# Splits, transposes and exchange of a four-head unit, each three steps further behind its loads

## The chip, the cores and the metric

The kernel runs on one core of a Trainium2 chip. The metric is the device time of one execution in microseconds (us); the times shown for a kernel are the median, lowest and highest of several runs. A trace of one execution shows for each engine (PE for matmuls, with its weight loads apart; DVE, ACT and POOL for elementwise work; SP, which here only issues DMAs) when each instruction ran and what it waited for.

## The reference

Block-causal attention over 8 batches of 8 heads with 576 positions of 64 elements, and behind it a mixture of experts in which each of the 4608 tokens goes to one of 8 experts.

```python
scores = scale * np.matmul(q, k.transpose(0, 1, 3, 2))
mask = block_i >= block_j                       # blocks of 64 positions
scores = np.where(mask, scores, -1000000000.0)
attn = softmax(scores)
x = np.matmul(attn, v)                          # then (batch*seq, heads*dim) = (4608, 512)

logits = x @ w_gate
e_idx = np.argmax(logits, axis=1)               # one expert for each token
eom = 1.0 / (1.0 + np.exp(-(x @ w_output_gate)))
for e in range(E):                              # 8 experts, w1 512x1024, w2 1024x512
    h = np.maximum(x[mask] @ w1[e], 0.0)
    out[mask] = gate_w[mask, None] * eom[mask, e, None] * (h @ w2[e])
```

## The kernel before

Attention comes first, the experts' matmuls after it. Attention goes through 32 *pairs* of heads (p = 0 to 31, four to a batch). For each pair the main loop (lines 936 to 964) calls `advance`, which weaves three generators: the scores and exponentials of pair p (`softmax`), the PE transposes of the probabilities of pair p-1 (`flip`), and the products with the values of pair p-2 (`values`). `weave_` (line 282) lets each generator take one step in turn, and after them each generator in the list `later`. `flip` has seven yields and so eight steps, hence a pair is eight *steps* long. The order on PE is the order in which these steps are written (a manual schedule). The instructions of the other engines and of the DMA queues are put in order by a planner at build time, which takes whatever its own model of the machine has ready, in the order of the program where several things are.

The q and k rows come in *units* of four heads (u = 0 to 15, two pairs each); unit u is first needed in the first step of pair 2u. The chain that prepares one unit is the class `Load` (lines 80 to 112):

- `fetch` (line 91): two DMAs of 576 KB on SP's queue, k and q, into two `nat` tiles (four buffers).
- `split(i)` (lines 96, 97): DVE casts `nat` to f16, POOL subtracts that from `nat` for the low part; both parts lie in one `sp` tile (two buffers).
- `turn(i)` (line 102): a DMA transpose on SP's queue, `sp` into `tr`.
- `swap` (lines 107, 108): two DMAs on SP's queue that copy the two halves of the transposed k crosswise into `sw`, the operand of the second score matmul (line 318).

`load_heads(u)` issues this chain. It is put into `later` at pair 2u-3 (for the last unit, 15, at pair 26), so it has three pairs, 24 steps, until its unit is needed. Its first step issues the fetch; an entry t of the tuple in line 123 means that the piece is issued in step t+1. Step 1 is in pair 2u-3, step 9 is the first of pair 2u-2, step 17 the first of pair 2u-1.

What else stands in SP's queue around these: `load_v` (line 293), called at the end of each pair, which issues four DMAs for that pair's values (`va` line 299, two for `vb` line 301, `v8` line 304; in the profile `v8` is `v`); and the stores of the attention rows `x_d` (line 460) of `finish_batch`, twelve further steps in `later` that run from pair 4b+6 on for batch b. The last step of `finish_batch` issues five scatters of the routing table on POOL (line 558). `load_first` (line 777) fetches and splits the weights of the first expert and gathers its tokens; it is put into `later` at the first pair that starts with all 16 units complete (line 948) and needs 24 steps. Unit 0 and unit 1 are prepared by `load_start`, with steps of its own.

Of the kernel before, what the change touches and what calls it, by code (L numbers as in the profile page):

```python
# [26 lines left out]
def block_attention_top1_moe(  # L27
# [86 lines left out]
    def load_heads(u):  # L114

        x = Load(u)
        x.fetch()
        todo = (
            lambda: x.split(0, nc.vector.tensor_copy, nc.gpsimd), lambda: x.split(1, nc.vector.tensor_copy, nc.gpsimd),
            lambda: x.turn(0), lambda: x.turn(1), x.swap,  # L120
        )
        at = 0
        for t, do in zip((4, 5, 8, 9, 13), todo):
            while at < t:
                at += 1
                yield
            do()
        x.done()
# [782 lines left out]


    loads = {2 * u - (4 if u == len(units) - 1 else 3): load_heads(u) for u in range(2, len(units))}
    loads[0] = start
    flips, prods = [], []
# [184 lines left out]
```

## Time and profile before

| | us |
|---|---|
| median of 3 runs | 831.13 |
| lowest, highest | 830.74, 835.34 |
| the profiled execution | 833.94 |
| its span, first to last instruction | 832.3 |
| PE busy in the span | 765.9 (92%) |
| DVE busy | 542.4 (65%) |
| ACT busy | 516.2 (62%) |
| POOL busy | 254.5 (31%) |

A row of a timeline in the sections below reads: start in us, length in us, engine, line, operation, output <- inputs, count; in square brackets stands how long the engine was idle before the row, and what ended that. A row of the waits reads: the engine and what it was about to do, <- what it waited for: us in total, times, longest. "SPq" is SP's queue, and its lengths are times of issue, not of the transfer. A row of the windows gives the stretch, its length, the busy time of PE, weight loads, DVE, ACT and POOL with the number of instructions in brackets, then the clock granted to PE (1.00 is full), the busy share of the DMA engines and GB/s. Attention takes the span up to about 402 us, the experts the rest.

### The profile page before, as it was taken

The numbers are of one execution on the slowest core, as the hardware profiler recorded it, in microseconds if no ns is written. First come the engines' busy times: TensorE is split into PE (matmuls) and PEld (weight loads), VectorE is DVE, ScalarE is ACT, GpSimd is POOL, SyncE is SP. The second block draws the span as 40 slices with busy tenths as digits, with TensorE's granted clock in tenths as the row PEclk, the third lists the DMA queues.
The fourth block names the chain that finished last, engine by engine and source line by source line (L and its number), as shares of the span: only waits on it lengthen the run. The fifth ranks groups of instructions, "written<-read, shape, count | busy, mean of one in ns | idle before, by whom it ended". The sixth has DMA issues, their size and how long they took to land. (4 is left out here: it accounts for less than half of the span.)

```text
span 832.3 us, 17653 instructions
## 1 busy us (share of the span) xinstructions
PE 765.9 (92%) x6430; PEld 512.0 (62%) x6430; DVE 542.4 (65%) x1192; ACT 516.2 (62%) x1206; POOL 254.5 (31%) x227
## 2 busy tenths in 40 slices
PE   4399997999899989788999999999999999999994
PEld 3266665656566656555676666676656666676652
DVE  5466874958587777858581866786566656786530
ACT  4478686776767767458512855775555555775530
POOL 4322142422324242437225542233122322210001
PEclk9789999999999999889999999999999999999998
DMA  8999989689689898995118699784789958832601
GB/s 156 177 181 169 188 119 174 154 177 221 137 170 189 152 186 172 201 233 165 41 59 278 157 278 328 240 253 101 236 267 296 291 172 251 192 52 58 225 30 41
DMA packets 258414, 149.13 MB, mean 179 GB/s; under 512 B 226960, under 2 KB 227024, under 8 KB 258320
## 3 DMA queue, kind: packets, MB, share of 16 engines
q1 hardware_dynamic: 250048, 128.64, 67.3%
q0 software_dynamic: 8272, 19.29, 7.4%
q8 instruction: 52, 0.85, 0.5%
q14 instruction: 42, 0.34, 0.1%
HBM read 122.23 MB, written 19.73 MB: 171 GB/s over the span
## 5 line engine op out<-in xcount | busy, mean ns | idle before, releaser
L873 PEld LDWEIGHTS <-w1b 128*128 128x128 f16 (+1 forms) x2112 | 182.7, 98 | 23.4 <-DVE w1b L762 1.5
L337 ACT ACTIVATE pt<-ps_s,nbs 128x448 f32<-128x448 f32 (+1 forms) x314 | 163.9, 531 | 34.1 <-DVE nbs L325 16.9
L873 PE MATMUL ps_s<-xt,w1b 128*128 128x256 f16 (+3 forms) x1824 | 182.1, 261 | 0.3 <-DVE w1b L762 0.2
L900 PE MATMUL ps_t<-w2b,hh 128*128 128x512 f16 x608 | 181.0, 379 | 1.3 <-ACT hh L881 1.3
L762 DVE TENSOR_TENSOR w2b<-w2f,w2b 128x1024 bf16<-128x1024 f32 x76 | 88.0, 1220 | 113.3 <-ACT w2b L761 113.3
L413 ACT COPY pT<-ps_t 128x512 f32<-128x512 f32 (+3 forms) x225 | 97.5, 461 | 74.9 <-PE ps_t L407 73.8
L407 PE MATMUL ps_t<-ident,pt 128*128 128x128 f32 (+1 forms) x800 | 128.9, 286 | 5.8 <-DVE xn L456 4.4
L97 POOL TENSOR_TENSOR sp<-nat,sp 128x1152 f16<-128x1152 f32 x30 | 71.2, 2375 | 147.6 <-DVE nbs L325 71.4
L900 PE MATMUL ps_t<-w2b,hl 128*128 128x512 f16 x304 | 115.2, 379 | 0.1
L317 PE MATMUL ps_s<-tr,tr 128*128 128x448 f16 (+1 forms) x378 | 100.0, 287 | 15.6 <-ACT pt L337 12.7
L903 ACT ACTIVATE ys<-ps_t,ids 128x512 f32<-128x512 f32 x38 | 26.1, 688 | 135.0 <-PE ps_t L900 115.6
L318 PE MATMUL ps_s<-sw,tr 128*128 128x448 f16 (+1 forms) x378 | 92.4, 286 | 13.3 <-DMA sw<-tr 13.2
L900 PEld LDWEIGHTS <-hh 128*128 128x128 f16 x608 | 59.2, 98 | 68.2 <-ACT hh L881 1.5
L904 POOL DMA_INDIRECT out_dram<-ys,ids x38 | 44.1, 1162 | 184.6 <-ACT ys L903 120.4
L407 PEld LDWEIGHTS ps_t<-ident,pt 128*128 128x128 f32 (+1 forms) x800 | 88.5, 144 | 18.7 <-DVE xn L456 4.8
L762 DVE TENSOR_TENSOR w1b<-w1f,w1b 128x1024 bf16<-128x1024 f32 x76 | 88.3, 1221 | 1.0 <-ACT w1b L761 0.7
L422 PE MATMUL ps_a<-pT,va 128*64 128x512 f32 (+3 forms) x256 | 84.5, 453 | 3.8 <-DMA va<-in_v_dram 3.6
L422 PE MATMUL ps_a<-pT,vb 128*64 128x512 f32 (+3 forms) x256 | 84.4, 453 | 1.0 <-DMA vb<-in_v_dram 1.0
L375 DVE TENSOR_REDUCE nmx<-ps_s 128x2 f32<-128x896 f32 (+1 forms) x63 | 60.2, 956 | 35.3 <-PE ps_s L320 35.0
L761 ACT CAST w1b<-w1f 128x1024 f16<-128x1024 f32 x76 | 74.4, 1045 | 2.6 <-DMA w1f<-in_moe_w_dram 2.6
L761 ACT CAST w2b<-w2f 128x1024 f16<-128x1024 f32 x76 | 73.6, 1042 | 0.0
L733 POOL DMA_INDIRECT xg<-x_d,ids x38 | 50.1, 1317 | 48.4 <-DMA ids<-tab_d 21.8
(196 smaller groups left out, 1084.7 us busy)
## 6 DMA issues: line engine op xcount, KB each, us to landing
w1f<-in_moe_w_dram SPq DMA_DIRECT2D x76, 512.0 KB
w2f<-in_moe_w_dram SPq DMA_DIRECT2D x76, 512.0 KB
nat<-in_k_dram SPq DMA_DIRECT2D x15, 576.0 KB
nat<-in_q_dram SPq DMA_DIRECT2D x15, 576.0 KB
sw<-tr SPq DMA_DIRECT2D x30, 288.0 KB
x_d<-xn SPq DMA_DIRECT2D x32, 256.0 KB
va<-in_v_dram SPq DMA_DIRECT2D x32, 128.0 KB
vb<-in_v_dram SPq DMA_DIRECT2D x64, 64.0 KB
```

The lines of the kernel that those rows point to most:

```text
L97: last_lo[0] = lo.tensor_tensor(sp[:, :, 1, :], self.nats[i], sp[:, :, 0, :], ALU.subtract)
L317: nc.tensor.matmul(ps_ap, qq, k1[ab][:, c0:c1], start=True, stop=False)
L318: nc.tensor.matmul(ps_ap, qq, k2[ab][:, c0:c1], start=False, stop=last)
L337: last_exp[0] = nc.scalar.activation(to, ap, AF.Exp, bias=nbs[0:r, t, ab:ab + 1], scale=SCALE, accum_out=sums[0:r, t, hA + ab:hA + ab + 1],)
L375: nc.vector.tensor_reduce(nmx[:, t, :], pX[:, :, 0:n], AX.X, ALU.max, negate=True)
L407: nc.tensor.transpose(ps[:, i, 0:rows], probs[t][0:rows, col:col + P], ident[0:rows, 0:rows])
L413: copies[next(nth)](pT[:, r:r + m, Q0[t]:Q0[t] + rows], ps[:, i:i + m, 0:rows])
L422: nc.tensor.matmul(pa[64 * a:64 * a + 64, P * j:512], (va, vb)[a][:, j, :], pT[:, 1 + 2 * j + a, 64 + P * j:576], start=(j == 0), stop=False,)
L761: nc.scalar.copy(hi, src)
L762: eng.tensor_tensor(lo, src, hi, ALU.subtract)
L873: nc.tensor.matmul(ph[:, f4].rearrange("p (h n) -> p h n", n=P), wv[:, cc, f, :], xv[:, cc], start=(k == 0), stop=(k == 3 * KD - 1))
L900: nc.tensor.matmul(py, hv[:, f, h], wv[:, f, :], start=(k == 0), stop=(k == 3 * KF - 1))
```

## The change

The tuple of steps in `load_heads` is changed: every piece behind the fetch is issued three steps later.

```diff
             lambda: x.turn(0), lambda: x.turn(1), x.swap,
         )
         at = 0
-        for t, do in zip((4, 5, 8, 9, 13), todo):
+        for t, do in zip((7, 8, 11, 12, 16), todo):
             while at < t:
                 at += 1
                 yield
             do()
         x.done()
```

| piece | step before | step after | |
|---|---|---|---|
| fetch | 1 | 1 | step 1 of pair 2u-3 |
| split 0, split 1 | 5, 6 | 8, 9 | from pair 2u-3 to its last step and the first of pair 2u-2 |
| turn 0, turn 1 | 9, 10 | 12, 13 | from steps 1, 2 of pair 2u-2 to steps 4, 5 |
| swap, done | 14 | 17 | from step 6 of pair 2u-2 to step 1 of pair 2u-1 |

For unit 15, which starts at pair 26, the last row means from pair 27 to pair 28, so that the test in line 948 is first met at pair 29 where it was met at pair 28. The work itself, its sizes and its buffers stay as they are.

## The prediction

> **What bounds the kernel now.** I read the page first (span, busy shares, slices), then the waits of PE within the attention stretch, then the stretch in windows, and last the timelines of SP, DVE, POOL and PE around single units. Below, pair p is the p-th run of `advance` (p = 0 to 31), unit u is needed by PE at the first step of p = 2u, and a step is one round of `weave_`, eight to a pair.
>
> ```profile
> span 832.3 us, 17653 instructions
> ...
> 42.00:402.00 360.00, 331.42 (x3102) 216.53 (x3101) 260.77 (x812) 262.80 (x862) 120.31 (x93) 0.97 0.88 174
> ...
> PE ps_s L318 <- DMA sw<-tr: 4.7, 3, 2.5
> PE ps_t L407 <- DVE xn L456: 4.4, 2, 3.9
> PE ps_a L422 <- DMA va<-in_v_dram: 3.6, 1, 3.6
> ```
>
> From 42 to 402 us, where the loads of the units run, PE is busy 331.4 of 360 us: PE bounds the stretch, with 28.6 us of idle time in it. Three of its waits there are for the exchanged operand `sw`, which is the last link of the moved chain, so for those units the chain is already the later of the two. Behind 402 us come the experts' matmuls, which the change doesn't touch; a delay in attention moves them as a whole and is paid in full.
>
> Idle PE costs twice, as these rows show (columns of the windows: length, busy time of PE, weight loads, DVE, ACT, POOL, then granted clock, DMA share, GB/s):
>
> ```profile
> 19.36 0.59 PE L317 MATMUL ps_s<-tr,tr 128*128 128x512 f16 x1 [2.89 <-ACT pt L337]
> 19.20:22.50 3.30, 3.14 (x19) 2.10 (x19) 3.27 (x8) 1.46 (x5) 2.60 (x2) 0.50 0.32 61
> 135.71 0.53 PE L317 MATMUL ps_s<-tr,tr 128*128 128x448 f16 x1 [4.13 <-ACT pt L337]
> 135.20:138.60 3.40, 2.89 (x12) 1.65 (x13) 2.40 (x5) 2.57 (x12) 2.70 (x2) 0.50 0.61 119
> 222.80:226.20 3.40, 0.96 (x12) 0.79 (x13) 0.44 (x2) 1.43 (x4) 0.00 (x0) 1.00 0.49 114
> 363.90:370.70 6.80, 5.90 (x19) 2.71 (x20) 1.04 (x3) 1.01 (x4) 3.57 (x4) 0.50 1.05 338
> ```
>
> After stalls of 2.89 and 4.13 us PE ran 3.3 to 3.4 us at half clock, after the 3.6 us wait for `va` 6.8 us; in and after a stall of 2.46 us (222.8 to 226.2) the clock stayed at 1.00. So a stall of about 2.9 us and more costs 1.7 us of PE time on top (half of 3.4), at worst 3.4.
>
> **The chain of one unit.** Unit 9, needed by pair 18:
>
> ```profile
> 202.11 0.19 PE L317 MATMUL ps_s<-tr,tr 128*128 128x64 f16 x1
> 204.11 0.94 POOL L558 DMA_INDIRECT tab_d<-idg,sli  x1 [6.65 <-DVE nbs L325]
> 205.16 0.70 DVE L96 CAST sp<-nat 128x1152 f16<-128x1152 f32 x1
> 206.48 0.54 SPq L304 DMA_DIRECT2D v<-in_v_dram  x1
> 210.81 2.39 POOL L97 TENSOR_TENSOR sp<-nat,sp 128x1152 f16<-128x1152 f32 x1
> 213.22 5.65 SPq L102 DMA_TRANSPOSE tr<-sp  x2
> 219.91 0.57 SPq L108 DMA_DIRECT2D sw<-tr  x1
> 220.53 1.98 SPq L299 DMA_DIRECT2D va<-in_v_dram  x1
> 224.55 0.47 SPq L91 DMA_DIRECT2D nat<-in_k_dram  x1
> 225.24 0.20 PE L318 MATMUL ps_s<-sw,tr 128*128 128x64 f16 x1 [2.46 <-DMA sw<-tr]
> ```
>
> Pair 16 starts at 202.11. POOL first issues five scatters of the routing table (from 204.11), then the second half of the split (210.81), so the transposes leave SP at 213.22, the second half of `sw` at 219.91, and PE, which wanted them for pair 18, gets going at 225.24: 23.1 us after pair 16 began, 5.33 us after that issue. The chain hangs on pair 16's own start (the scatters wait for DVE work of that pair), so later PE work gives it no air. Two more things: the splits were due in pair 15 (steps 5 and 6) and the transposes in steps 1 and 2 of pair 16, yet they ran after 205 and 213: everything runs more than three steps behind its program step already. And SP takes its work in the order of the program: exchange of u, values of pair 2u-2, fetch of u+1.
>
> **The change, part by part.** No instruction is added or taken away. *Splits* (DVE L96, POOL L97): due steps 8 and 9 for 5 and 6. As they run later than that now, I cost them at nothing; the cover is the lateness, and if the planner does place them later they lengthen the chain by up to 4.7 us a unit (three steps of the 12.5 us a pair, 402/32, divided by 8), or free DVE from a wait (rival 1). *Transposes*: steps 4 and 5 of pair 2u-2 for 1 and 2. On SP they pass nothing: the values of that pair come at its end. Nothing, on the same cover and with the same bound.
>
> *Exchange*: from step 6 of pair 2u-2 to step 1 of pair 2u-1. That moves it past the end of pair 2u-2, where `load_v` puts four DMAs into SP's queue (and, in every other unit, past one `x_d` store). It stays ahead of the fetch of the next unit, so the fetch leaves SP in the same place; queued behind the exchange are fetch and next values as before. The exchange leaves later by what SP takes for the four, from the `va` row to the `nat` row: unit 9, 224.55 - 220.53 = 4.02 us. The other units whose exchange PE waits for, or nearly:
>
> ```profile
> 177.19 0.20 PE L318 MATMUL ps_s<-sw,tr 128*128 128x64 f16 x1 [1.40 <-DMA sw<-tr]
> 173.41 0.90 SPq L299 DMA_DIRECT2D va<-in_v_dram  x1
> 176.99 0.47 SPq L91 DMA_DIRECT2D nat<-in_k_dram  x1
> 271.93 0.20 PE L318 MATMUL ps_s<-sw,tr 128*128 128x64 f16 x1 [0.89 <-DMA sw<-tr]
> 266.91 0.86 SPq L299 DMA_DIRECT2D va<-in_v_dram  x1
> 270.51 0.46 SPq L91 DMA_DIRECT2D nat<-in_k_dram  x1
> 314.21 0.58 SPq L108 DMA_DIRECT2D sw<-tr  x1
> 314.84 0.90 SPq L299 DMA_DIRECT2D va<-in_v_dram  x1
> 318.48 0.46 SPq L91 DMA_DIRECT2D nat<-in_k_dram  x1
> 318.81 0.19 PE L318 MATMUL ps_s<-sw,tr 128*128 128x64 f16 x1
> ```
>
> Unit 7: 3.58 us, unit 11: 3.60, unit 13: 3.64 (no stall yet, but its exchange left only 4.60 us before PE took it, so there is no slack). With unit 9 that is 14.8 us, all on the path. Bounds: 0, if the values slip into time in which SP waits anyway, and 14.8, since nothing else moves past. I take 14.8, as the rows are these very DMAs.
>
> *Clock.* The stalls become 1.40+3.58 = 5.0, 2.46+4.02 = 6.5, 0.89+3.60 = 4.5 and about 3.6 us. All are above 2.9, so four drops at 1.7 us: 6.8 us; between 0 and 13.6 (two windows each). The Trainium skill, "TensorE: Matmul & The Clock Gate", part 1, says that the clock halves after an idle window of about 3.4 us which runs free of the kernel; a stall of 3.6 to 6.5 us would then cover a whole window only by chance, an estimated 1.7 times of four, 3 us for 6.8. The trace speaks against that reading: 2.89 us of idle time were enough.
>
> *Even units* also pass one store. Unit 10:
>
> ```profile
> 242.14 0.60 SPq L108 DMA_DIRECT2D sw<-tr  x1
> 242.84 0.72 SPq L460 DMA_DIRECT2D x_d<-xn  x1
> 247.81 0.43 SPq L91 DMA_DIRECT2D nat<-in_k_dram  x1
> 249.95 0.19 PE L318 MATMUL ps_s<-sw,tr 128*128 128x64 f16 x1
> ```
>
> Landed at about 242.14 + 5.33 = 247.5, needed at 249.95: 2.5 us of air. It moves by 4.5 us (242.84 to 247.81 less the last store, some 0.4). It would be late by 2.0, of which the slow clock after the odd unit's stall takes 1.7 (PE itself is later). I take 0.3 for each of units 8, 10 and 12: 0.9; bounds 0 and 6.0.
>
> *Ends of the row.* Units 2 to 4 and 6 have the exchange many microseconds ahead: nothing. Unit 5's delay is followed by the 4.13 us stall of pair 10 on a fetch that doesn't move, and goes into it: nothing, between -1.7 (its slow clock gone) and +2.9. For unit 15 the values of pair 27 now leave ahead of the exchange:
>
> ```profile
> 355.89 0.54 SPq L107 DMA_DIRECT2D sw<-tr  x1
> 357.12 1.32 SPq L299 DMA_DIRECT2D va<-in_v_dram  x1
> 393.15 2.12 POOL L762 TENSOR_TENSOR w2b<-hl,w2b 128x1024 bf16<-128x1024 f32 x1
> 418.33 0.27 PE L873 MATMUL ps_s<-xh,w1b 128*128 128x256 f16 x1
> ```
>
> That is 1.2 us earlier for `va`: the 3.6 us stall falls to 2.4, and without its drop 3.4 us of PE time come back: -4.6; between 0 and -7.0. Unit 15 is complete in pair 28 for 27, so `load_first` starts at pair 29, a pair (some 12 us) later. Its last split ended at 395.3, PE's first expert matmul came at 418.3: covered. Without that cover it would cost up to those 12 us. Unit 14, whose transposes now come behind the fetch of unit 15: nothing, between -7.3 (the 3.9 us stall for `xn` and its slow clock) and +4.5.
>
> Sum: 14.8 + 6.8 + 0.9 - 4.6 = 17.9 us on the profiled execution (833.94 us). The median of the runs shown is 831.13, 2.8 lower; the gain or loss is set on it: 849.
>
> **The rivals.** *1, faster.* The splits really move behind the next pair's `nmx`, and DVE no longer stands before them:
>
> ```profile
> 132.66 0.76 DVE L96 CAST sp<-nat 128x1152 f16<-128x1152 f32 x1 [6.03 <-DMA nat<-in_k_dram]
> ```
>
> Here DVE stood 6.03 us for a fetch, and PE lost the 4.13 us of 135.71 with 1.7 of clock; the stall of 3.9 for `xn` with up to 3.4 is of the same kind. Gain 13.1: 818. It decides only if the exchanges still land in time, so the order on SP must not change as I say. Against it: the splits follow their data, not their step. *2, nothing.* The planner keeps its order, or the values fill time in which SP waits for POOL (before unit 9's transposes SP issues nothing from 206.48 + 0.54 to 213.22): 831. Against it: the transposes were due long before the values. *3, much slower.* Every drop takes two windows and the even units miss too: 14.8 + 13.6 + 6.0 = 34: 866.
>
> **How the numbers follow.** Forecast 0.58, rival 1 0.13, rival 2 0.20, rival 3 0.09. One per cent, 8.3 us, is about what can be told from no change. Forecast and rival 3 make slower 0.67; rival 2 makes 0.20 the same; rival 1 makes 0.13 faster. The likeliest case alone runs from 842 (two drops of four, the full 7.0 us back at the end: 14.8 + 3.4 - 7.0 = 11.2) to 861 (two windows a drop, even units late: 14.8 + 13.6 + 6.0 - 4.6 = 29.8). The range 826 to 862 takes in rival 2 and leaves out rival 3 and most of rival 1.
>
> **What would show it.** Right: on SP the four value DMAs stand between transposes and `sw`; PE's wait for `sw` goes from 4.7 us in three to about 20 in four or more; more windows at 0.50. Wrong: `sw` right behind the transposes, or L96 behind the next pair's L354 and no wait of DVE for `nat`, or a late `load_first` seen as a wait of L873 or L900 for `w1b` or `w2b`.

## The result and the profile after

| | us |
|---|---|
| before, median of 4 runs | 831.51 (830.74 to 835.34) |
| after, median of 4 runs | 841.12 (838.77 to 842.94) |
| ratio after/before, 95% interval | 1.0106 [1.0066, 1.0146] |
| profiled execution after | 838.77 |

The changed kernel is slower by 1.1%, 9.6 us. The profiled execution is the fastest of its four and 4.8 us above that of before, so its trace holds about half of the difference; what the other half is has to come from more executions (below). From the page of after, the span and the line of busy times:

```profile
span 837.1 us, 17614 instructions
...
PE 768.7 (92%) x6406; PEld 513.5 (61%) x6430; DVE 547.2 (65%) x1182; ACT 520.3 (62%) x1216; POOL 257.2 (31%) x227
```

DVE, which was given nothing new to do, is busy 4.8 us longer than the 542.4 before. That is the first hint that something stretches its instructions. Next the waits of PE in the same stretch as before, 42 to 402 us, of after:

```profile
PE ps_s L317 <- ACT pt L337: 13.7, 8, 3.8
PE ps_s L318 <- DMA sw<-tr: 9.4, 3, 4.5
PE ps_t L407 <- DVE xn L456: 4.4, 3, 2.4
```

The wait for `sw` doubled, from 4.7 to 9.4 us, and the one for `va` (3.6 us before) is gone. It did not become 20 us in four waits, as the prediction said. The order on SP is the one it worked with. Unit 9 in the timeline of SP's queue, after:

```profile
214.32 5.68 SPq L102 DMA_TRANSPOSE tr<-sp  x2
220.05 0.58 SPq L299 DMA_DIRECT2D va<-in_v_dram  x1
220.68 1.30 SPq L301 DMA_DIRECT2D vb<-in_v_dram  x2
222.35 0.56 SPq L304 DMA_DIRECT2D v<-in_v_dram  x1
223.01 0.54 SPq L107 DMA_DIRECT2D sw<-tr  x1
223.60 0.58 SPq L108 DMA_DIRECT2D sw<-tr  x1
224.23 0.77 SPq L91 DMA_DIRECT2D nat<-in_k_dram  x1
```

The four value DMAs stand between the transposes and `sw`, and take 223.01 - 220.05 = 2.96 us there (4.02 was taken). Four long stalls of PE come in after (timeline of PE):

```profile
177.53 0.20 PE L318 MATMUL ps_s<-sw,tr 128*128 128x64 f16 x1 [3.49 <-DMA sw<-tr]
...
228.32 0.21 PE L318 MATMUL ps_s<-sw,tr 128*128 128x64 f16 x1 [4.46 <-DMA sw<-tr]
...
268.51 0.21 PE L317 MATMUL ps_s<-tr,tr 128*128 128x64 f16 x1 [3.75 <-ACT pt L337]
...
318.22 0.19 PE L317 MATMUL ps_s<-tr,tr 128*128 128x64 f16 x1 [3.70 <-ACT pt L337]
```

The first two are the waits for `sw` of units 7 and 9. The other two come one pair ahead of units 11 and 13, at the first score matmul of that pair, and are for exponentials; what stands ahead of those is shown further below. Now the windows, first of after, then of before (columns as in the prediction):

```profile
42.00:389.00 347.00, 320.40 (x2994) 208.03 (x2994) 247.41 (x766) 255.82 (x842) 105.48 (x81) 0.97 0.88 170
389.00:423.90 34.90, 29.61 (x255) 18.95 (x255) 24.82 (x60) 19.47 (x50) 19.79 (x14) 0.95 0.37 108
178.60:182.00 3.40, 3.40 (x14) 1.06 (x12) 1.17 (x7) 1.60 (x9) 0.00 (x0) 0.51 1.35 220
226.40:233.20 6.80, 4.88 (x22) 2.34 (x23) 1.55 (x7) 1.60 (x9) 0.00 (x0) 0.50 1.26 221
267.40:274.20 6.80, 5.69 (x26) 2.94 (x26) 2.21 (x12) 3.16 (x13) 1.25 (x1) 0.50 0.98 189
318.60:322.00 3.40, 3.40 (x13) 1.15 (x10) 1.55 (x7) 1.89 (x11) 0.00 (x0) 0.50 1.06 197
```

```profile
42.00:389.00 347.00, 320.61 (x2999) 209.28 (x2998) 248.06 (x778) 253.90 (x833) 115.60 (x89) 0.97 0.90 177
389.00:418.30 29.30, 26.73 (x254) 17.28 (x252) 19.40 (x57) 17.27 (x49) 9.62 (x9) 1.00 0.18 53
343.40:350.20 6.80, 5.01 (x33) 4.10 (x34) 3.85 (x11) 2.66 (x6) 4.29 (x3) 0.50 0.79 184
```

In both kernels pair 31 starts at 389.0 us (388.84 and 388.99), after the same 320 us of PE and at the same mean clock of 0.97. Within attention these two executions lost nothing to each other. The four stalls each brought a slow clock, 3.4 + 6.8 + 6.8 + 3.4 = 20.4 us at half speed; but before had its own in this stretch, 3.4 us at 135.2, 6.8 at 343.4 and 6.8 at 363.9, and all three are gone (the one at 135.2 for a reason that has nothing to do with the change, see below). What differs is the piece behind it: from 389.0 to the first matmul of the experts (L873) after takes 34.9 us where before took 29.3, and in it PE is idle 34.9 - 29.6 = 5.3 us instead of 2.6, and its clock falls to 0.95. POOL is busy 19.8 us in it instead of 9.6. The longest wait of PE there and the slow clock behind it, after:

```profile
395.95 0.66 PE L407 MATMUL ps_t<-ident,pt 128*128 128x128 f32 x4 [2.36 <-DVE xn L456]
...
397.10:400.50 3.40, 3.28 (x14) 2.27 (x14) 2.01 (x4) 2.17 (x8) 1.58 (x1) 0.50 0.92 310
```

PE waits for `xn` (L456), which stands on DVE right behind an instruction of L497 that took 4.66 us (its rows are in the last section). The weights of the first expert were ready in time: POOL's last subtraction for them ends at 420.53, 3.35 us before the first matmul of L873 (423.88), which has no wait in front of it.

### The profile page after: what moved, and what is told of

The parts are those of the page before. It is cut to its first block, busy times and chain, and to the rows that moved or that the text cites. A ratio compares the mean times of both kernels' runs of the same rounds, so it can differ in the third digit from the quotient of the medians.

```text
span 837.1 us, 17614 instructions
## 1 busy us (share of the span) xinstructions
PE 768.7 (92%) x6406; PEld 513.5 (61%) x6430; DVE 547.2 (65%) x1182; ACT 520.3 (62%) x1216; POOL 257.2 (31%) x227
## 5 line engine op out<-in xcount | busy, mean ns | idle before, releaser
L873 PEld LDWEIGHTS <-w1b 128*128 128x128 f16 (+1 forms) x2112 | 182.5, 98 | 24.0 <-DVE w1b L762 1.5
L337 ACT ACTIVATE pt<-ps_s,nbs 128x448 f32<-128x448 f32 (+1 forms) x314 | 163.8, 531 | 33.2 <-DVE nmx L354 13.8
L873 PE MATMUL ps_s<-xt,w1b 128*128 128x256 f16 (+3 forms) x1824 | 182.1, 261 | 0.8 <-DVE w1b L762 0.4
L900 PE MATMUL ps_t<-w2b,hh 128*128 128x512 f16 (+1 forms) x584 | 175.8, 379 | 0.0
L762 DVE TENSOR_TENSOR w2b<-w2f,w2b 128x1024 bf16<-128x1024 f32 x76 | 88.1, 1221 | 113.4 <-ACT w2b L761 113.4
L317 PE MATMUL ps_s<-tr,tr 128*128 128x448 f16 (+1 forms) x378 | 100.3, 289 | 19.5 <-ACT pt L337 17.2
L903 ACT ACTIVATE ys<-ps_t,ids 128x512 f32<-128x512 f32 x38 | 26.1, 687 | 135.7 <-PE ps_t L900 116.0
L318 PE MATMUL ps_s<-sw,tr 128*128 128x448 f16 (+1 forms) x378 | 92.9, 289 | 17.3 <-DMA sw<-tr 17.3
L762 DVE TENSOR_TENSOR w1b<-w1f,w1b 128x1024 bf16<-128x1024 f32 x76 | 88.1, 1217 | 0.5 <-ACT w1b L761 0.5
L422 PE MATMUL ps_a<-pT,va 128*64 128x512 f32 (+3 forms) x256 | 87.1, 464 | 0.0
L422 PE MATMUL ps_a<-pT,vb 128*64 128x512 f32 (+3 forms) x256 | 87.1, 463 | 0.0
L733 POOL DMA_INDIRECT xg<-x_d,ids x38 | 52.7, 1388 | 52.0 <-DMA ids<-tab_d 19.2
```

The source lines that it names most:

```text
L317: nc.tensor.matmul(ps_ap, qq, k1[ab][:, c0:c1], start=True, stop=False)
L318: nc.tensor.matmul(ps_ap, qq, k2[ab][:, c0:c1], start=False, stop=last)
L337: last_exp[0] = nc.scalar.activation(to, ap, AF.Exp, bias=nbs[0:r, t, ab:ab + 1], scale=SCALE, accum_out=sums[0:r, t, hA + ab:hA + ab + 1],)
L422: nc.tensor.matmul(pa[64 * a:64 * a + 64, P * j:512], (va, vb)[a][:, j, :], pT[:, 1 + 2 * j + a, 64 + P * j:576], start=(j == 0), stop=False,)
L762: eng.tensor_tensor(lo, src, hi, ALU.subtract)
L873: nc.tensor.matmul(ph[:, f4].rearrange("p (h n) -> p h n", n=P), wv[:, cc, f, :], xv[:, cc], start=(k == 0), stop=(k == 3 * KD - 1))
```

## The experiments

Times of the same kernel differed between the three groups of runs (before had medians of 841.8, 841.0 and 831.7 us), so only ratios to the before of the same group are compared. All diffs are against the kernel before, where the text doesn't name the changed one. "Step" counts as in the table of the change: the tuple entry t is step t+1, and the exchange is at step 14 before and 17 after. "Weights at 28" or "at 29" is the pair at which `load_first` starts.

**First group.** Theories: the exchange behind the values (the prediction's), against the later start of `load_first`.

### e1_exchange_alone

```diff
-        for t, do in zip((4, 5, 8, 9, 13), todo):
+        for t, do in zip((4, 5, 8, 9, 16), todo):
```

> Steps (4, 5, 8, 9, 16): only the exchange is moved behind the values of its pair; splits and transposes stay. Theory A (the exchange's new place in SP's queue makes the loss before pair 28): the attention part loses as in the changed kernel, stalls for sw of 3.5 us and more at pairs 14 and 18 with slow clock, and with the later start of the expert weights the whole is slower by 8 to 10 us, about 840. Theory C (the later splits and transposes make the loss, since the second cast then meets POOL's subtraction at units 11 and 13): no cast above 2 us, the loss about 7 us a pair of them smaller, about 832 to 835.

Measured 1.0127 [1.0104, 1.0149], 851.81 us. The moved exchange, with the weights at 29 that follow from it, costs the whole of the change or more. That is the size of theory A, but not its stalls: PE's only wait for `sw` from 42 to 402 us is one of 2.5 us at pair 14, and at pairs 17, 21 and 25 it waits 3.6, 2.3 and 2.9 us for exponentials, with no cast above 2 us. So such stalls come without the stretched casts of theory C.

### e2_exchange_before_values

```diff
-        for t, do in zip((4, 5, 8, 9, 13), todo):
+        for t, do in zip((7, 8, 11, 12, 15), todo):
```

> Steps (7, 8, 11, 12, 15): as the changed kernel, but the exchange one step earlier, which puts it ahead of the values of pair 2u-2 on SP again and leaves the start of the expert weights at pair 28. Theory A: no loss, 829 to 833; sw right behind the transposes, PE's waits for sw as before. Theory C: the two stretched casts at units 11 and 13 stay, with two stalls of 3.7 us and slow clock; 836 to 842.

Measured 1.0023 [1.0005, 1.0041], 843.53 us. One step less for the exchange puts it ahead of the values again and the weights back to 28, and about four fifths of the 1.1% are gone. Its waits of PE from 42 to 402 us:

```profile
PE ps_a L422 <- DMA va<-in_v_dram: 3.3, 1, 3.3
...
PE ps_s L318 <- DMA sw<-tr: 1.9, 2, 1.2
```

The wait for `va` is back, the one for `sw` is small. But two things changed at once here; e3 and e4 part them.

### e3_after_weights_at_28

The changed kernel, with the weights started at pair 28 as before:

```diff
-        if len(loaded) == len(units) and not w1b:
+        if p == 28 and not w1b:
```

> The changed kernel with the expert weights started at pair 28 as before, whatever unit 15 does. Theory B (the pair by which the first expert's weights start later costs what is lost behind pair 31): pair 31 to the first expert matmul is 29.5 us again instead of 34.9, but the gain of 6.7 us between pairs 28 and 30 goes if it came from the weights being out of the way: 836 to 841. If that gain came from the values of pair 27 leaving ahead of the exchange, it stays and the whole is 834 to 836.

Measured 0.9998 [0.9977, 1.0019], 841.82 us. With the exchange behind the values but the weights at 28, nothing is lost, which is less than either expectation had. This is against the prediction's theory.

### e4_before_weights_at_29

The kernel before, with the weights a pair later:

```diff
-        if len(loaded) == len(units) and not w1b:
+        if p == 29 and not w1b:
```

> The kernel before with the expert weights started at pair 29. Theory B: about 5 us lost behind pair 31, so 836 if nothing comes back between pairs 28 and 30, and 829 to 831 if the weights' transfers at pair 28 made the 3.6 us wait for values and its slow clock. My prediction had this at no cost.

Measured 1.0046 [1.0026, 1.0065], 845.19 us. The later start alone costs, about half as much as the whole change.

**Second group.** What makes the later start dear? In the trace of after, POOL's subtractions for the split weights (L762) fall beside the routing arithmetic of batch 6 on DVE (L497 to L547). The theory: they hold DVE up.

### f1_after_again

The changed kernel once more, to compare the others of this group with.

> The changed kernel itself, so that it stands on one chip with the next three. All theories: about 1.01 of the kernel before.

Measured 1.0077 [1.0046, 1.0107], 847.5 us.

### f4_after_first_splits_on_dve

The changed kernel, weights at 29, with the eight subtractions of the first expert on DVE instead of POOL (line 801):

```diff
-                    fn(nc.gpsimd, 0, wc[c], c)
+                    fn(nc.vector, 0, wc[c], c)
```

> The changed kernel with the low halves of the first expert's weights subtracted on DVE instead of POOL (eight of about 1.2 us for eight of 2.1 us). Theory D (the later start costs because POOL's subtractions now fall beside the routing arithmetic of batch 6 on DVE, whose instructions with two inputs then stand still until POOL is done: 4.66 us for one that takes 0.49): no DVE instruction of L497 to L547 above 1 us, most of the loss gone, 1.000 to 1.004. If the lateness itself or ACT's casts cost, it stays at 1.008 or more, and the 10 us of work on DVE come on top.

Measured 0.9993 [0.9963, 1.0022], 841.4 us. DVE has more to do, and the loss is gone, with the weights still at 29. The times of the stretched instruction show it; the view of line 497 gives count, then shortest/median/longest in ns. First after, then e4, then f4:

```profile
L497 DVE TENSOR_TENSOR lh<-lh x16: 307/406/4660, 95.2 to 425.2; 128x320 f32<-128x320 f32 x8, 128x160 f32<-128x160 f32 x8
```

```profile
L497 DVE TENSOR_TENSOR lh<-lh x16: 308/404/3185, 95.0 to 431.1; 128x320 f32<-128x320 f32 x8, 128x160 f32<-128x160 f32 x8
```

```profile
L497 DVE TENSOR_TENSOR lh<-lh x16: 315/404/493, 96.2 to 429.9; 128x320 f32<-128x320 f32 x8, 128x160 f32<-128x160 f32 x8
```

The two kernels with weights at 29 and subtractions on POOL have one instruction of 4.7 and 3.2 us among those of 0.4; with the subtractions on DVE the longest is 0.49.

### f3_exchange_alone_28

e1 with the weights back at 28:

```diff
-        for t, do in zip((4, 5, 8, 9, 13), todo):
+        for t, do in zip((4, 5, 8, 9, 16), todo):
...
-        if len(loaded) == len(units) and not w1b:
+        if p == 28 and not w1b:
```

> Steps (4, 5, 8, 9, 16) and the expert weights started at pair 28: the exchange behind the values of its pair and nothing else. Theory A (the exchange's place costs, my 14.8 us and 6.8 us of clock): 1.010 or more. Theory B (nearly all of the loss is the pair by which the expert weights start later): 0.998 to 1.004, with waits for sw longer than before but made good elsewhere.

Measured 1.0072 [1.0044, 1.0100], 845.59 us, between the two expectations. So the exchange alone does cost, 0.7%, where splits and transposes stay early; with them late too (e3) it costs nothing. The parts don't add up, and that stays open.

### f5_after_28_first_half_on_act

The changed kernel with weights at 28, and the casts of the units on ACT, to take DVE's casts from beside POOL's subtractions:

```diff
-            lambda: x.split(0, nc.vector.tensor_copy, nc.gpsimd), lambda: x.split(1, nc.vector.tensor_copy, nc.gpsimd),
+            lambda: x.split(0, nc.scalar.copy, nc.gpsimd), lambda: x.split(1, nc.scalar.copy, nc.gpsimd),
...
-        if len(loaded) == len(units) and not w1b:
+        if p == 28 and not w1b:
```

> The changed kernel with the expert weights at pair 28 and the first half of each split (the cast) on ACT instead of DVE. If casts of DVE that stand still beside POOL's subtraction (3.4 us for 0.75, each with a stall of PE near 3.7 us and slow clock) are what is left of the loss in attention, this beats the kernel before: 0.990 to 0.996, no stall of PE of 3 us behind a cast. If not, ACT's extra work (28 casts) costs: 1.000 to 1.006.

Measured 1.0136 [1.0097, 1.0175], 850.58 us: a miss. No cast of a unit stands still any more (1.14 to 1.19 us each on ACT), and the stalls at the starts of pairs 21 and 25, 3.75 and 3.70 us in after, are down to 0.45 us each. But PE now waits for `sw` six times, among them 2.15 and 2.18 us for units 11 and 13, for which after has no such wait:

```profile
PE ps_s L318 <- DMA sw<-tr: 9.3, 6, 2.6
```

**Third group.** Is there a gain in the splits and transposes alone, or in taking subtractions off POOL?

### g1_splits_and_turns_alone

```diff
-        for t, do in zip((4, 5, 8, 9, 13), todo):
+        for t, do in zip((7, 8, 11, 12, 13), todo):
```

> Steps (7, 8, 11, 12, 13): splits and transposes three steps later, the exchange and the start of the expert weights where they were. So far the exchange alone (weights at pair 28) stands at 1.007 and all together (weights at pair 28) at 1.000. Theory E (the later splits and transposes are a gain that pays for the exchange): 0.992 to 0.997. Theory F (the exchange's cost is a matter of how waits and casts happen to fall, not a sum of parts): 0.999 to 1.003, as the kernel with the exchange at step 16 of 24 (1.002).

Measured 1.0004 [0.9978, 1.0030], 831.79 us: no difference. In its waits of PE from 42 to 402 us the one for `sw` stands where it stood before the change (4.7 us in three):

```profile
PE ps_s L318 <- DMA sw<-tr: 4.6, 3, 2.4
...
PE ps_a L422 <- DMA va<-in_v_dram: 3.1, 1, 3.1
```

### g2_before_first_splits_on_dve

The edit of f4 on the kernel before (weights at 28).

> The kernel before with the low halves of the first expert's weights on DVE. Theory D: the two routing instructions that stand still 1.3 and 1.5 us beside POOL at pair 31 go, 0.996 to 0.999; as weights at pair 28 meet less of the routing work, the gain is smaller than the 0.8 per cent that the same edit brought in the changed kernel. If DVE's extra 10 us of work tell: 1.000 to 1.003.

Measured 1.0034 [1.0006, 1.0062], 834.29 us: a miss as a gain, but it makes f4 plain. In before, where POOL's subtractions hold DVE up less (L498 takes 1.58 us and L506 1.68, usually 0.22 and 0.18), moving them to DVE costs 0.3%; in the changed kernel the same edit took 0.8% off. So f4 didn't gain by the edit as such.

### g3_after_28_first_lo_on_dve

The changed kernel with weights at 28, and the low half of each unit's first split on DVE instead of POOL:

```diff
-            last_lo[0] = lo.tensor_tensor(sp[:, :, 1, :], self.nats[i], sp[:, :, 0, :], ALU.subtract)
+            ins = lo.tensor_tensor(sp[:, :, 1, :], self.nats[i], sp[:, :, 0, :], ALU.subtract)
+            if lo is nc.gpsimd:
+                last_lo[0] = ins
...
-            lambda: x.split(0, nc.vector.tensor_copy, nc.gpsimd), lambda: x.split(1, nc.vector.tensor_copy, nc.gpsimd),
+            lambda: x.split(0, nc.vector.tensor_copy, nc.vector), lambda: x.split(1, nc.vector.tensor_copy, nc.gpsimd),
```

> The changed kernel with the expert weights at pair 28 and the low half of the first of the two splits on DVE instead of POOL, so that for odd units the first transpose no longer stands behind the five scatters on POOL. If the chain from the pair's start through the scatters sets when sw lands (my reading of unit 9), the first transpose of odd units comes some 4 us and the second 2.4 us earlier, PE's waits for sw go below 1 us, and DVE's casts meet no subtraction of POOL: 0.990 to 0.997. If DVE's 15 further instructions cost more than the chain gives: 1.000 to 1.006.

Measured 1.0189 [1.0148, 1.0230], 845.73 us: a miss, and the slowest of all. The exponentials come late instead (the edit adds two lines, so its L319 is L317 elsewhere; waits of PE, 42 to 402 us):

```profile
PE ps_s L319 <- ACT pt L339: 20.9, 15, 2.8
```

### g4_splits_turns_and_dve

The tuple of g1 with the edit of f4.

> Steps (7, 8, 11, 12, 13) with the first expert's low halves on DVE: the sum of the two runs above if they are independent. A candidate that beats both kernels if theory D and theory E hold: 0.988 to 0.996; with theory F 0.996 to 1.001.

Measured 1.0044 [1.0017, 1.0071], 835.5 us: a miss, in line with g2. No kernel tried here is faster than the one before.

### All profiled executions in three stretches

One execution says little to within a few us, so here are all of them with the loads on the engines of before (without f5 and g3, which change those). The times are read from the timelines of PE: when the first matmul of L318 of pairs 12, 26 and 30 starts, and the first of pair 31 (L317) and of the experts (L873).

| exchange | kernel | pair 12 to 26 | 26 to 30 |
|---|---|---|---|
| step 14 or 16, ahead of the values | before, e2, e4, g1, g2, g4 | 162.2, 169.9, 171.1, 165.9, 166.0, 162.1 | 58.2, 58.3, 54.8, 57.3, 60.5, 60.6 |
| step 17, behind them | after, f1, e1, e3, f3, f4 | 175.6, 177.5, 175.5, 174.5, 176.8, 177.1 | 47.9, 49.5, 51.4, 49.1, 53.3, 49.3 |
| difference of the means | | +10.0 | -8.2 |

| weights, subtractions | kernel | pair 31 to L873 |
|---|---|---|
| at 29, on POOL | after, f1, e1, e4 | 34.9, 39.7, 37.8, 36.6 |
| at 28, on POOL | before, e2, e3, f3, g1 | 29.5, 33.2, 33.0, 33.1, 31.1 |
| on DVE, at 28 or 29 | g2 (28), g4 (28), f4 (29) | 30.2, 30.2, 30.2 |

In the first table the two groups overlap in neither column; in the second the first row lies above the other two. The exchange behind the values costs 10.0 us from pair 12 to 26 and gives 8.2 back by pair 30. The weights at 29 on POOL cost 37.3 - 32.0 = 5.3 us behind pair 31 (means of the first two rows). The sum, 7.1 us, stands against 9.6 measured. How far one execution goes: e4 has the loads of before and takes 171.1 us from pair 12 to 26 where before takes 162.2, so before's own trace lies at the fast end there.

The same executions show that the place of the exchange also changes the order that the planner gives to DVE. With the exchange at step 17 the second cast of units 11 and 13 stands ahead of both maxima (L386) that the last exponentials of the pair wait for; at step 14 or 16 at least one maximum goes first. Unit 11 on DVE, first after, then before:

```profile
262.78 3.42 DVE L96 CAST sp<-nat 128x1152 f16<-128x1152 f32 x1
266.12 1.41 DVE L386 TENSOR_REDUCE nmx<-ps_s 128x1 f32<-128x576 f32 x2
```

```profile
258.39 0.76 DVE L386 TENSOR_REDUCE nmx<-ps_s 128x1 f32<-128x576 f32 x1
259.07 1.23 DVE L96 CAST sp<-nat 128x1152 f16<-128x1152 f32 x1
...
260.28 0.74 DVE L386 TENSOR_REDUCE nmx<-ps_s 128x1 f32<-128x576 f32 x1
```

How long PE then stalls for exponentials (us, `pt` of L337) at the start of the next pair:

| exchange | kernel | pair 21 | pair 25 |
|---|---|---|---|
| step 14 or 16 | before, e2, e4, g1, g2, g4 | 0.91, 0.86, 0.86, 0.91, 0.91, 0.92 | none |
| step 17 | after, f1, e1, e3, f3, f4 | 3.75, 2.96, 2.30, 1.30, 2.01, 2.53 | 3.70, 2.82, 2.92, 2.91, 2.83, 3.06 |

With the casts on ACT (f5, exchange at step 17) it is 0.45 us at both. So these stalls need the cast on DVE; how much of them is its place and how much something else is not shown.

## Why the prediction was right, and where it was not

The direction held and the time lies in the range. The shift was forecast as 17.9 us and is 9.6. By the steps of the sum:

- **Order on SP**: right. The values stand between transposes and `sw`, and the fetch of the next unit keeps its place.
- **Exchange in the odd units, 14.8 us, clock, 6.8, and even units, 0.9**: 22.5 us together, and 13.4 in the profiled execution. Pair 12 to pair 26, from the first L318 matmul of the one to that of the other, first after, then before:

```profile
153.73:329.33 175.60, 157.62 (x1446) 101.71 (x1444) 122.80 (x375) 123.51 (x408) 55.89 (x43) 0.94 0.83 162
```

```profile
156.58:318.81 162.23, 151.24 (x1446) 99.02 (x1444) 119.19 (x381) 121.17 (x402) 55.77 (x43) 1.00 0.88 172
```

  - *Clock*: the same 1446 matmuls keep PE busy 6.4 us longer, close to the 6.8. Four drops came, as predicted, though two of them not at the waits that were named, and with six windows of 3.4 us where four were taken (8 was the upper bound).
  - *Exchange*: this term is too large. In the intervals that end with units 7, 9, 11 and 13 (each from the first L318 matmul of one unit to that of the next), idle time of PE grew by 3.1, 2.1, 2.0 and 2.5 us (forecast 3.58, 4.02, 3.60 and 3.64), 9.6 us together. For units 7 and 9 the mechanism is the one predicted, a longer wait for `sw`. For 11 and 13 it is not: PE stalls a pair earlier, for exponentials, where the second cast now stands ahead of the maxima on DVE, and no wait for `sw` is left. The prediction took DVE's order as unchanged, so that these two come out at half to two thirds of their forecast is luck. f5, with the casts off DVE, does wait for `sw` at both (2.15 and 2.18 us).
  - *Even units*: in the intervals of units 8, 10 and 12 idle time fell by 2.6 us instead of growing by 0.9. Part of the matmuls made longer by the slow clock went into idle time that had been there.
- **Ends of the row**: unit 5 was put at nothing, with -1.7 as its best case; after reaches pair 12 2.9 us earlier than before, since the stall at pair 10 fell from 4.13 us to 1.2 and its slow clock went. That is chance: from pair 10 to pair 12 the trace of before takes 29.7 us and the eleven others of the tables above 23.9 to 26.1, e4 and g2 with the loads of before among them (25.7 both). Unit 14 was put at nothing and gave 3.2 (the stall of 3.9 for `xn` with its slow clock is gone). Unit 15 was right in kind: the values of pair 27 leave first, the wait for `va` vanishes (it is there, with 2.7 to 3.9 us, in all six executions with the exchange at step 14 or 16, and in none of the six at step 17), and 7.2 us come back, the forecast's best case of 7.0 rather than its 4.6. The forecast counted every drop of the clock that would come, but of those that would go only the one behind `va`. By pair 30, losses and gains are even in this execution (377.19 against 377.04), thanks to the 2.9 us of chance; over all of them 1.8 us of loss are left from pair 12 on.
- **Splits and transposes, nothing**: right by themselves. Alone they make 1.0004 (g1), and rival 1 doesn't happen.
- **`load_first` a pair later, "covered: nothing"**: this is the step that failed. It asked only whether the weights would be ready for the first expert, and they were. It did not ask whom POOL's work would run beside. With the exchange behind the values but the weights at 28 the ratio is 0.9998 (e3); with nothing but the weights at 29 it is 1.0046 (e4); with the weights at 29 and the subtractions off POOL it is 0.9993, in the same group of runs as after's 1.0077 (f4, f1), though that edit alone costs 0.3% (g2). That the loss of the changed kernel hangs on these subtractions running then and there is shown: it goes when they start earlier and when they leave POOL.

So the prediction reached the right side by adding a loss in attention that was mostly given back (1.8 us left from pair 12 to 30), and missing the one behind pair 31, 5.3 us, that is more than half of what is measured. That the time lies in its range is in good part luck. Rival 2 ("nothing") was nearer for attention than the forecast, though not by its own reason: the order did change.

Open is why the exchange alone with early splits costs 0.7% (f3, weights at 28) and together with late splits nothing (e3). The profiled f3 reaches pair 30 6.9 us behind e3 (383.8 and 376.9), though they were not of one group. Open is also why the subtractions cost 0.3% on DVE at pair 28.

## What to carry to other kernels

A piece of work that is moved may start something else through a test on a list or a counter; follow that too, and ask not only whether its result comes in time, but beside which engine's work it will now run. An order changed on one queue can change the planner's order on another engine too; a forecast that takes that as fixed should say so. When stalls are costed with the slow clock behind them, count the ones that go as carefully as those that come, and treat the price read off one wait as a bound: the next slack gives part of it back.

## What the runs showed of the hardware

Some DVE instructions stand still while POOL runs a tensor operation. First the view of line 96 of after (shortest/median/longest in ns), then rows from its timeline of DVE:

```profile
L96 DVE CAST sp<-nat x30: 695/756/3420, 17.2 to 350.2; 128x1152 f16<-128x1152 f32 x30
```

```profile
262.78 3.42 DVE L96 CAST sp<-nat 128x1152 f16<-128x1152 f32 x1
...
390.63 4.66 DVE L497 TENSOR_TENSOR lh<-lh 128x320 f32<-128x320 f32 x1
...
399.27 1.83 DVE L507 TENSOR_TENSOR eq<-eq,erev 128x40 f32<-128x40 f32 x1
```

Beside them POOL, after:

```profile
263.19 2.39 POOL L97 TENSOR_TENSOR sp<-nat,sp 128x1152 f16<-128x1152 f32 x1
...
390.74 2.12 POOL L762 TENSOR_TENSOR w1b<-hh,w1b 128x1024 bf16<-128x1024 f32 x1
392.83 2.11 POOL L762 TENSOR_TENSOR w1b<-hl,w1b 128x1024 bf16<-128x1024 f32 x1
...
398.92 2.13 POOL L762 TENSOR_TENSOR w2b<-hh,w2b 128x1024 bf16<-128x1024 f32 x1 [2.12 <-ACT w2b L761]
```

And before, where L497 has no subtraction beside it and L498 has one, from DVE and then POOL:

```profile
390.35 0.48 DVE L497 TENSOR_TENSOR lh<-lh 128x320 f32<-128x320 f32 x1
...
391.11 0.68 DVE L456 TENSOR_TENSOR xn<-ps_t,rec 128x512 f32<-128x512 f32 x1
391.71 1.58 DVE L498 TENSOR_TENSOR L<-lh 128x80 f32<-128x80 f32 x1
```

```profile
391.01 2.18 POOL L762 TENSOR_TENSOR w2b<-hh,w2b 128x1024 bf16<-128x1024 f32 x1 [2.21 <-DMA x_d<-xn]
```

L497 ends at 395.29, 0.35 us after the second of two subtractions (392.83 + 2.11 = 394.94): it stood through both, 4.66 us for 0.48. L507 ends at 401.10, POOL at 401.05. In before, L498 (both inputs `lh`) takes 1.58 us, 0.22 in after, and ends 0.10 us behind POOL; L456, which reads `ps_t`, goes beside the same subtraction at its usual length, 0.68. The cast takes 3.42 us for its usual 0.75 and ends 0.62 us behind POOL's subtraction, which began 0.41 us after it. Behind that cast come the maxima that ACT needs for the exponentials, and behind those the stall of 3.75 us at 268.51; a stretched cast at 312.54 (3.37 us) stands in the same way ahead of the one of 3.70 at 318.22. The stretch is not all of these stalls: in f1, the same kernel, the two casts take 1.47 and 1.31 us, and PE still stalls 2.96 and 2.82 us.

The Trainium skill, "SBUF — State Buffer", section "SBUF: two separate sides", says that of a DVE instruction with two inputs in SBUF and a GpSimd instruction that reads SBUF the one that starts first holds the port pair they share for its whole length, and that the other is blocked in full. The trace agrees for L497, with the 4.66 us against 0.48; it adds that POOL's next instruction can go ahead of the DVE instruction that waits. The cast has one input, so that sentence doesn't cover it, and by the rows it began first; why it stood is not shown here.

All four stalls of after of 3.49 to 4.46 us were followed by half clock, one or two windows of 3.4 us. In the fourteen profiled executions, from 46 to 432 us, each of the 30 stalls of PE of 2.82 us and more was followed by half clock within 3.6 us of its end, and so were 28 of the 49 from 1.9 to 2.81 us. So the prediction's 2.9 us is a length from which the drop was sure here, and not one below which it stays away. The strict reading of the Trainium skill, "TensorE: Matmul & The Clock Gate", part 1, that the prediction weighed (an idle window that runs free must be covered whole, an estimated 1.7 drops of four) is not borne out here.
